# Taking the branch to a rarely used part behind the last scatter, with its flag copied there by GpSimd

## The chip, the cores and the metric

The kernel runs on one core of one Trainium2 chip. The metric is the device time of one execution in microseconds, taken as the median of several runs. The core has five engines that run their own instruction streams and wait for each other by semaphores: TensorE (PE; its weight loads are shown as PEld), VectorE (DVE), ScalarE (ACT), GpSimd (POOL) and SyncE (SP). A name with a q, such as POOLq, is that engine's sequencer: the part that takes instructions in order, waits for semaphores, loads registers, branches, and hands the rest to the engine.

## The reference, cut to what matters

A causal convolution of seven taps runs over 8 sequences of 2880 tokens with 192 features, with weights from a softmax for each of 8 heads. Its 23040 result rows go through a mixture of experts: each token picks one of 4 groups and one of the group's 4 experts by the largest logit, and is put through that expert alone.

```python
for k in range(K):                       # K = 7 taps, w = softmax(weight) per head
    out[b, s] += w[h, k] * x_pad[b, s + k]
g_idx = argmax(x @ w_group); e_idx = argmax(xg @ w_expert[g])
h  = maximum(xg[mask_e] @ w1[g, e], 0.0) # 192 -> 1024
ye = h @ w2[g, e]                        # 1024 -> 192
out[tok_idx] = combined[:, None] * ye    # weight of group times weight of expert
```

## The kernel before, in words

The first stage goes over the tokens in 18 units of 4 to 12 blocks of 120 tokens. For each unit TensorE does the convolution with a banded matrix and the router's logits; VectorE picks the expert, counts each token's place in its expert's list and builds the list; GpSimd writes the list to a table in DRAM with an indirect DMA (`idtab`), and ScalarE's queue writes the convolved rows (`xcd`).

The second stage works in slots of 256 tokens of one expert. For each slot GpSimd gathers the rows by an indirect DMA (`gather`, line 653), TensorE turns them (`turn`), multiplies by the first matrix (`hidden`, line 684) and the second (`back`, lines 702 and 706); the operands are split into a high and a low part, which is work for ScalarE and VectorE (lines 618 to 634, 689 and 690; line 627 is on GpSimd in the tail). `finish` (lines 753 to 757) scales the result: ScalarE writes one part of `ys`, VectorE adds the other, and GpSimd scatters each half of a slot (128 rows) to the output by an indirect DMA. The list of slots, `plan`, has three portions of fixed slots and a tail of 18 entries (9 of 256 and 9 of 128 tokens) that a table, computed on the chip in `table`, fills with what is left over. 187 scatters run in all: 160 for the portions, 27 for the tail (`idpt`).

Should the tail's 18 entries not be enough, or a list overflow, a flag (`flagi`, written by VectorE in line 878) is set, and a part at the program's end does the rest. That part is under `tc.If`: two loops whose code for all engines stands behind the branch. With this data the flag is 0, and the branch skips it. Every engine has the branch in its own stream, and so loads the flag into a register by itself (a TENSOR_LOAD), compares and branches. On the other side of the branch, each engine raises its semaphores to the values that the skipped part would have left; on GpSimd that includes one instruction for the semaphores of its DMAs, INC_SWDGE_SEM. The program ends with a DRAIN on each engine and a barrier (line 1233).

The order within an engine's stream is made by a scheduler, save where the code pins it (`tc.keep_in_program_order`). In the code, the flag is loaded six plan entries before the end (line 1106), ahead of the loop's last entries; the streams that the scheduler makes have the load and the branch near the end of each engine's work, and GpSimd's last scatter stands behind the branch.

Of the kernel before, what the change touches and what calls it, by code (L numbers as in the profile page):

```python
# [13 lines left out]
I32 = mybir.dt.int32  # L14
# [18 lines left out]
OOB_WHY = "the table's entries are clamped by construction"  # L33
# [3 lines left out]
def conv_moe_kernel(  # L37
# [10 lines left out]
    nc = tc.nc  # L48
# [106 lines left out]
    const = ctx.enter_context(tc.tile_pool(name="const", bufs=1))  # L155
# [90 lines left out]
    def clear_table():  # L246
# [12 lines left out]
        out=tri, in_=ones, pattern=[[1, P]], compare_op=ALU.is_gt, fill=0.0, base=0, channel_multiplier=-1,  # L259
# [12 lines left out]
    for nb in sorted({n for _, n in units}):  # L272
# [35 lines left out]
        out=sel, in_=ident.rearrange("p (e l) -> p e l", e=E), axis=AX.X, op=ALU.add)  # L308
    nc.gpsimd.iota(io[:, 0:1], pattern=[[0, 1]], base=0, channel_multiplier=1)
    nc.vector.tensor_scalar(  # L310
        out=io[:, 1:2], in0=io[:, 0:1], scalar1=LE - 1, scalar2=None, op0=ALU.bitwise_and)
# [6 lines left out]
    for g in range(NSK):  # L318
        nc.sync.dma_start(
            out=skew[0:R, g * HG:(g + 1) * HG],  # L320
            in_=bass.AP(wvd.tensor, wvd.offset + VL - KS - (BT - 1) + g * HG * VL, [[1, R], [VL, HG], [1, VW]]),
# [13 lines left out]
    for h in range(H):  # L335
        nc.scalar.activation(
            out=band[0:R, h], in_=skew[0:R, h, BT - 1::-1], func=AF.Exp, bias=wm[0:R, h:h + 1],
# [338 lines left out]
    def hidden(W, X, f2, hook=lambda: None):  # L676
        xa, xb = X
        ah, al, bh, bl = (W[n] for n in ("ah", "al", "bh", "bl"))
        hp = ph.tile([P, 2, SLOT], F32, name="ph")
        for j in range(2):  # L680
            fs = slice((2 * f2 + j) * P, (2 * f2 + j + 1) * P)
            ops = ((ah, xa[:, 0]), (al, xa[:, 0]), (ah, xa[:, 1]), (bh, xb), (bl, xb))
            for i, (wgt, xx) in enumerate(ops):
                nc.tensor.matmul(out=hp[:, j], lhsT=wgt[:, fs], rhs=xx, start=i == 0, stop=i == len(ops) - 1)  # L684
            if j == 0:
                hook()
        hh = ff.tile([P, 2, SLOT], F32R, name="hh", bufs=HB)
        hl = ff.tile([P, 2, SLOT], F32R, name="hl", bufs=HB)
        nc.scalar.activation(out=hh, in_=hp, func=AF.Relu)  # L689
        nc.vector.scalar_tensor_tensor(  # L690
            out=hl, in0=hp, scalar=0.0, in1=hh.bitcast(F32), op0=ALU.max, op1=ALU.subtract,
        )
        return hh, hl
# [84 lines left out]
    flagi = const.tile([P, 2], I32, name="flagi")  # L778
# [166 lines left out]
    def advance(rate):  # L945
        credit[0] += rate
        while credit[0] >= 1.0:
            credit[0] -= 1.0
            step()

    tab = [None]
    nrare = [None]
# [55 lines left out]
    plan = [(pi, e, s) for pi, (_, spe) in enumerate(portions) for e in range(E) for s in range(spe)]  # L1008
# [9 lines left out]
    def tiles(i):  # L1018

        return 1 if plan[i][0] == "tail" and plan[i][1] >= NBIG else 2  # L1020
# [74 lines left out]
    def later(lag, f):  # L1095

        pend.append((tick + lag, f))
        pend.sort(key=lambda a: a[0])
# [3 lines left out]
            pend.pop(0)[1]()  # L1102

    for i, (pi, e, s) in enumerate(plan):
        if i == len(plan) - 6:
            nrare[0] = nc.values_load(
                flagi[0:1, 1:2], min_val=0, max_val=1, skip_runtime_bounds_check_because=OOB_WHY)
        W, ids = opened[i]
        n = tiles(i)
        oo = [po.tile([P, 512], F32, name="po") for _ in range(n)]  # L1110
        steps = NF // 2 if n == 2 else 2
        for f2 in range(steps):
            last = f2 == steps - 1
            if n == 2:
                HH = hidden(W, turned[i], f2, lambda: advance(rate[0]))
                advance(rate[0])

                def fold(W=W, oo=oo, HH=HH, f2=f2, ids=ids, xs=gathered[i], last=last):
                    back(W, oo, HH, f2, lambda: advance(rate[0]))
                    if last:  # L1120
                        finish(oo, ids, xs)

                later(LAG - last, fold)
            else:
                hr = hidden_small(W, turned[i], f2)

                def fold(W=W, oo=oo, hr=hr, f2=f2, ids=ids, xs=gathered[i], last=last):
                    HH = turn_small(hr)

                    def fold2():  # L1130
                        back_small(W, oo, HH, f2)
                        if last:
                            finish(oo, ids, xs)

                    later(LAG_S, fold2)

                later(0.5, fold)
            if f2 == 0:
                open_slot(i + 2)
            for q in range(f2, NF // 2, steps):  # L1140
                k = (q + 2) % 4
                if q < 2:
                    split_one(W, k)
                elif i + 1 < len(plan):
                    split_one(opened[i + 1][0], k)
            if i + 1 < len(plan):
                if f2 == n - 1:
                    turned[i + 1] = turn(gathered[i + 1], tiles(i + 1))
            drain(tick)
            tick += 1  # L1150
# [2 lines left out]
        drain(tick)  # L1153


    with tc.If(nrare[0] != 0):
        nover = nc.values_load(
            flagi[0:1, 0:1], min_val=0, max_val=1, skip_runtime_bounds_check_because=OOB_WHY)
        with tc.For_i(0, nover, 1):
            for u in range(NU):  # L1160
                c0, nb = units[u]
                ee = rt.tile([P, UB, E], F32, name="dd")[0:BT, 0:nb]
                gi = rt.tile([P, 2, UB], I32, name="posi", bufs=1)[0:BT, :, 0:nb]
                gb = rt.tile([P, 2, UB], F32, name="posb")[0:BT, :, 0:nb]
                gr = rt.tile([P, UB], F32, name="posr", bufs=1)[0:BT, 0:nb]
                idw = rt.tile([P, LH], I32, name="lsi")[0:BT, 0:nb]
                pn = posn[0:BT, c0:c0 + nb]
                va = vals[0:BT, 0:nb]
                nc.vector.tensor_copy(out=gi[:, 1], in_=pn)
                nc.vector.tensor_scalar(  # L1170
                    out=gi[:, 0], in0=gi[:, 1], scalar1=VS.bit_length() - 1, scalar2=None, op0=ALU.logical_shift_right)
                nc.vector.tensor_scalar(out=gi[:, 1], in0=gi[:, 1], scalar1=VS - 1, scalar2=None, op0=ALU.bitwise_and)
                nc.vector.tensor_copy(out=gb, in_=gi)
                nc.vector.tensor_scalar(out=gb[:, 0], in0=gb[:, 0], scalar1=float(VS), scalar2=-1.0, op0=ALU.mult, op1=ALU.add)
                nc.vector.tensor_tensor(
                    out=ee, in0=eoff[0:BT].unsqueeze(1).broadcast_to([BT, nb, E]),
                    in1=gb[:, 0].unsqueeze(2).broadcast_to([BT, nb, E]), op=ALU.is_equal,
                )
                nc.vector.tensor_tensor(
                    out=ee, in0=ee, in1=ends[0:BT, u].unsqueeze(1).broadcast_to([BT, nb, E]), op=ALU.mult)  # L1180
                nc.vector.tensor_reduce(out=gr, in_=ee, axis=AX.X, op=ALU.add)
                nc.vector.tensor_tensor(out=gr, in0=gr, in1=gb[:, 1], op=ALU.add)
                nc.vector.tensor_copy(out=gi[:, 0], in_=gr)
                nc.vector.tensor_scalar(out=idw, in0=va, scalar1=float(c0 * BT - 1), scalar2=None, op0=ALU.add)
                for k in range(nb):
                    nc.gpsimd.indirect_dma_start(
                        out=idtab[:, :], out_offset=bass.IndirectOffsetOnAxis(ap=gi[:, 0, k:k + 1].bitcast(U32), axis=0),
                        in_=idw[:, k:k + 1], in_offset=None,
                    )
            for _ in table(ebase, 0, 0):  # L1190
                pass
        nend[0] = nc.values_load(
            tab[0][0:1, 0, 3:4], min_val=NTAIL, max_val=NTAB, skip_runtime_bounds_check_because=OOB_WHY,
        )
        with tc.For_i(NTAIL, nend[0], 1) as i:
            r1, r2, row = tail_regs(lambda c: tab[0][0:1, bass.ds(i, 1), c:c + 1], 3)
            W = weights(r1, r2)
            ids = ff.tile([P, 2, 1], I32, name="idt", bufs=1)
            tail_ids(row, ids)
            while W["todo"]:  # L1200
                split_one(W)
            xs = gather(ids, N)
            X = turn(xs)
            oo = [po.tile([P, 512], F32, name="po") for _ in range(2)]
            HHs = []
            for f2 in range(NF // 2):
                HHs.append(hidden(W, X, f2))
                if f2:
                    back(W, oo, HHs[f2 - 1], f2 - 1)
            back(W, oo, HHs[-1], NF // 2 - 1)  # L1210
            finish(oo, ids, xs)
# [25 lines left out]
```

## Time and profile before

| what | value |
|---|---|
| median of 3 runs | 1174.79 us (1172.58 to 1176.51) |
| the profiled execution's own time | 1170.84 us |
| its span, first to last instruction | 1169.0 us |
| mean granted TensorE clock | 0.977 |
| TensorE busy | 1111.7 us (95%) |
| VectorE, ScalarE, GpSimd busy | 69%, 59%, 43% |
| last stretch without any matmul | 1155 to 1169 us |

Engine times in the profile do not count what the sequencers do: register loads, branches, semaphore steps and drains. Those are listed only in the view of a source line, each as queue, operation, count, duration in ns (least, median, greatest), and the first and last start in us. The end of this kernel has to be read from there, since the busy engines are done by then. Spans on GpSimd are rough.

### The profile page before, as it was taken

To read this page: it belongs to the slowest core of one execution; us is meant where nothing else is said; L and a number is where in the kernel's file an instruction comes from. 1 tells how busy PE (TensorE), PEld (TensorE's weight loads), DVE (VectorE), ACT (ScalarE), POOL (GpSimd) and SP (SyncE) were. 2 spreads that over 40 slices of the span, in tenths; PEclk is the share of its full clock that TensorE was granted. 3 is DMA by queue.
4 is the path that set the end of the run, shared out by engine and by line. 5 is a ranking of instruction groups with operands and counts; after the bars stand their busy time and mean duration, and the time that the engine had idled before them with its cause. 6 is when DMAs were issued, how large, how long until landed. Compare 5 with 4: busy or idle time off the path is not lost.

```text
span 1169.0 us, 23803 instructions
## 1 busy us (share of the span) xinstructions
PE 1111.7 (95%) x8468; PEld 1079.3 (92%) x8468; DVE 804.5 (69%) x1668; ACT 690.1 (59%) x1374; POOL 498.2 (43%) x443
## 2 busy tenths in 40 slices
PE   5887999999999999999999999999999999999994
PEld 4766999998999999999999999999999999998984
DVE  4756788887877676666678565656565656688772
ACT  5544677657655555656554555555555656677772
POOL 2103234434434343434344444444444445578771
PEclk8879999999999999999999999999999999999997
DMA  8766699989775654546354574545454545599960
GB/s 228 217 182 178 173 213 230 226 203 268 217 194 143 165 156 118 143 116 170 95 162 95 155 203 128 142 128 141 130 141 128 140 118 167 146 243 266 248 160 19
DMA packets 167212, 195.63 MB, mean 167 GB/s; under 512 B 22500, under 2 KB 144333, under 8 KB 167086
## 3 DMA queue, kind: packets, MB, share of 16 engines
q1 hardware_dynamic: 125006, 140.41, 44.6%
q0 software_dynamic: 18752, 35.85, 10.5%
q10 hardware_dynamic: 23328, 17.80, 6.2%
q8 instruction: 67, 1.10, 0.4%
q14 instruction: 59, 0.48, 0.1%
HBM read 158.79 MB, written 36.58 MB: 167 GB/s over the span
## 4 chain that ended last, share of the span: by engine, by line
PE 79%; DVE 5%; DMA 4%; issue 3%; ACT 3%; another core or an unknown queue 0%; POOL 0%; POOLq 0%; ACTq 0%; DVEq 0%; SPq 0%
PE ph L684 33%; PE po L702 21%; PE po L706 10%; PE pm L409 3%; DMA xg<-xcd,idpt 3%; PE pm L451 2%; PE pm L666 2%; PE pm L667 2%; PE pm L428 1%; PE ph L719 1%; PE pm L448 1%; DVE hl L690 1%; DVE ohl L549 1%; DMA idtab<-lsi,rowi 1%; ACT cw L633 1%
## 5 line engine op out<-in xcount | busy, mean ns | idle before, releaser
L702 PE MATMUL po<-cw,hh 128*128 128x384 f32 x1424 | 443.4, 369 | 5.9 <-DVE ys L754 5.9
L684 PE MATMUL ph<-xa,ah 128*128 128x256 f32 x1424 | 390.2, 296 | 1.9 <-DVE xa L669 1.5
L757 POOL DMA_INDIRECT out<-ys,idp x160 | 167.8, 1049 | 447.4 <-DVE ys L754 348.8
L706 PE MATMUL po<-cw,hl 128*128 128x192 f32 x1424 | 357.3, 251 | 0.0
L690 DVE SCALAR_TENSOR_TENSOR hl<-ph,hh 128x512 fp32r<-128x512 f32 x356 | 241.2, 686 | 163.5 <-ACT hh L689 149.3
L689 ACT ACTIVATE hh<-ph 128x512 fp32r<-128x512 f32 x356 | 210.8, 594 | 205.8 <-PE ph L684 170.2
L702 PEld LDWEIGHTS po<-cw,hh 128*128 128x128 f32 x1424 | 268.6, 189 | 9.7 <-DVE ys L754 7.6
L684 PEld LDWEIGHTS ph<-xa,ah 128*128 128x128 f32 x1424 | 271.0, 190 | 5.0 <-DVE xa L669 1.6
L706 PEld LDWEIGHTS po<-cw,hl 128*128 128x128 f32 x1424 | 272.6, 191 | 1.5
L653 POOL DMA_INDIRECT xg<-xcd,idp x160 | 190.0, 1187 | 62.0 <-issue 29.6
L684 PE MATMUL ph<-xb,bh 128*128 128x256 f32 x712 | 201.9, 284 | 0.3 <-DVE xb L673 0.3
L684 PE MATMUL ph<-xb,bl 128*128 128x256 f32 x712 | 201.8, 283 | 0.0
L684 PE MATMUL ph<-xa,al 128*128 128x256 f32 x712 | 201.3, 283 | 0.0
L684 PEld LDWEIGHTS ph<-xa,al 128*128 128x128 f32 x712 | 136.5, 192 | 2.1
L684 PEld LDWEIGHTS ph<-xb,bl 128*128 128x128 f32 x712 | 136.7, 192 | 0.0
L684 PEld LDWEIGHTS ph<-xb,bh 128*128 128x128 f32 x712 | 136.2, 191 | 0.4 <-DVE xb L673 0.4
L634 DVE TENSOR_TENSOR cw<-rawc,cw 128x768 fp32r<-128x768 f32 x114 | 105.3, 953 | 18.3 <-ACT cw L633 13.7
L619 DVE TENSOR_TENSOR al<-raw,ah 128x1024 fp32r<-128x1024 f32 x57 | 70.5, 1238 | 38.8 <-ACT ah L618 21.6
L754 DVE SCALAR_TENSOR_TENSOR ys<-po,xg,ys 128x192 f32<-128x192 f32 x187 | 76.2, 416 | 23.2 <-ACT ys L753 18.1
L633 ACT ACTIVATE cw<-rawc 128x768 fp32r<-128x768 f32 x114 | 91.0, 837 | 1.8 <-DMA rawc<-in_moe_w 1.4
L672 ACT ACTIVATE xb<-pm 64x256 fp32r<-64x256 f32 x98 | 36.0, 367 | 93.4 <-DVE xa L669 86.2
L753 ACT ACTIVATE ys<-po,xg 128x192 f32<-128x192 f32 x187 | 75.8, 418 | 22.2 <-PE po L706 12.0
(216 smaller groups left out, 1561.0 us busy)
## 6 DMA issues: line engine op xcount, KB each, us to landing
rawc<-in_moe_w SPq DMA_DIRECT2D x114, 384.0 KB
raw<-in_moe_w SPq DMA_DIRECT2D x57, 512.0 KB
raw<-in_moe_w SPq DMA_DIRECT2D x114, 256.0 KB
xcd<-xc ACTq DMA_DIRECT2D x13, 1085.6 KB
xin<-in_x SPq DMA_DIRECT2D x7, 1134.0 KB
xc<-in_moe_w SPq DMA_DIRECT2D x18, 384.0 KB
xin<-in_x SPq DMA_DIRECT2D x6, 1039.5 KB
xin<-in_moe_w SPq DMA_DIRECT2D x9, 512.0 KB
```

The source lines that it names most:

```text
L619: eng.get(k, nc.vector).tensor_tensor(out=al, in0=ra, in1=ah.bitcast(F32), op=ALU.subtract)
L633: pin(PINW, nc.scalar.activation(out=cw[:, fs, 0, :], in_=rc[k - 2], func=AF.Copy))
L634: eng.get(k, nc.vector).tensor_tensor(out=cw[:, fs, 1, :], in0=rc[k - 2], in1=cw[:, fs, 0, :].bitcast(F32), op=ALU.subtract,)
L653: nc.gpsimd.indirect_dma_start(out=xs[:, t, :], out_offset=None, in_=xcd[0:known, :], in_offset=bass.IndirectOffsetOnAxis(ap=ids[:, t, 0:1 ...
L684: nc.tensor.matmul(out=hp[:, j], lhsT=wgt[:, fs], rhs=xx, start=i == 0, stop=i == len(ops) - 1)
L689: nc.scalar.activation(out=hh, in_=hp, func=AF.Relu)
L690: nc.vector.scalar_tensor_tensor(out=hl, in0=hp, scalar=0.0, in1=hh.bitcast(F32), op0=ALU.max, op1=ALU.subtract,)
L702: nc.tensor.matmul(out=oo[t][:, 0:2 * D], lhsT=hh[:, j, ts], rhs=cw[:, f].rearrange("p a d -> p (a d)"), start=f == 0, stop=False,)
L706: nc.tensor.matmul(out=oo[t][:, 0:D], lhsT=hl[:, j, ts], rhs=cw[:, f, 0, :], start=False, stop=f == NF - 1,)
L753: nc.scalar.activation(out=ys[:, t, :], in_=oo[t][:, D:2 * D], func=AF.Copy, scale=g)
L754: nc.vector.scalar_tensor_tensor(out=ys[:, t, :], in0=oo[t][:, 0:D], scalar=g, in1=ys[:, t, :], op0=ALU.mult, op1=ALU.add,)
L757: nc.gpsimd.indirect_dma_start(out=outviews[nscat[0] % len(outviews)], out_offset=bass.IndirectOffsetOnAxis(ap=ids[:, t, 0:1].bitcast(U32) ...
```

## The change

Two lines go and three come. The flag is no longer loaded six entries before the end. Behind the loop, GpSimd copies the first row of `flagi` (two numbers) into a tile of its own, `flagl`; the copy is pinned in program order, which on GpSimd puts it behind the loop's last scatter. All five engines then load the flag from `flagl`, so each load needs the copy's semaphore. The branch, the part behind it and the end of the program are as they were.

```diff
     for i, (pi, e, s) in enumerate(plan):
-        if i == len(plan) - 6:
-            nrare[0] = nc.values_load(
-                flagi[0:1, 1:2], min_val=0, max_val=1, skip_runtime_bounds_check_because=OOB_WHY)
         W, ids = opened[i]
...
+    flagl = const.tile([1, 2], I32, name="flagl")
+    tc.keep_in_program_order(nc.gpsimd.tensor_copy(out=flagl, in_=flagi[0:1]))
+    nrare[0] = nc.values_load(flagl[0:1, 1:2], min_val=0, max_val=1, skip_runtime_bounds_check_because=OOB_WHY)
     with tc.If(nrare[0] != 0):
```

GpSimd's stream around the branch, as a difference (`-` before, `+` now). `bl` is a low part of the tail's weights, `out<-ys,idpt` a scatter of the tail, line 1157 the first instruction of the rarely used part:

```order
 L627 TENSOR_TENSOR bl<-xin,bh 128x1024
 L627 TENSOR_TENSOR bl<-raw,bh 128x1024
-L757 DMA out<-ys,idpt 23040x192 x5
-L1106 TENSOR_LOAD flagi
+L757 DMA out<-ys,idpt 23040x192 x6
+L1154 COPY flagl<-flagi 1x2
+L1155 TENSOR_LOAD flagl
 L1156 COMPARE_AND_BRANCH
 L1157 TENSOR_LOAD flagi
```

All six last scatters now stand ahead of the branch, with the copy and the load between. The other piece of GpSimd's stream is its end, on the branch's other side (the first row is INC_SWDGE_SEM):

```order
 L1156 ISA
 L1156 UNCONDITIONAL_BRANCH
-L757 DMA out<-ys,idpt 23040x192
-L1233 UNCONDITIONAL_BRANCH
 L1233 ISA
```

The sixth scatter stood here, and is gone from here. On VectorE the load and the branch stay behind the last `ys`, and the load reads the other tile:

```order
 L731 TENSOR_TENSOR hl<-pm,hh 128x512
 L754 SCALAR_TENSOR_TENSOR ys<-po,xg_202,ys 128x192
-L1106 TENSOR_LOAD flagi
+L1155 TENSOR_LOAD flagl
 L1156 COMPARE_AND_BRANCH
 L1157 TENSOR_LOAD flagi
```

Nothing of VectorE's work is moved there; the other engines' streams differ in the same way. Apart from this, one small instruction moves in the whole program: near the tail's table, VectorE's cast of line 874 goes ahead of an operation of line 690 and one of line 669.

## The prediction

> **What bounds the kernel now.** I read the page first: TensorE is busy almost everywhere, so the middle of the kernel is its matmuls, and this change touches none of them. What matters is what stands behind the last matmul. The view that sums busy time by stretch shows it.
>
> ```profile
> PE 1111.7 (95%) x8468; PEld 1079.3 (92%) x8468; DVE 804.5 (69%) x1668; ACT 690.1 (59%) x1374; POOL 498.2 (43%) x443
> ...
> 1146.00:1155.00 9.00, 7.94 (x53) 7.31 (x52) 2.64 (x5) 3.54 (x7) 1.94 (x2) 1.00 0.06 19
> 1155.00:1169.00 14.00, 0.00 (x0) 0.00 (x0) 0.00 (x0) 0.00 (x0) 0.97 (x1) 0.55 0.02 6
> ```
>
> In the last 14.0 us no matmul, vector or activation instruction runs; only one GpSimd instruction does, 0.97 us long. The timeline says which (start, length, engine, line), with the last matmuls and two of the VectorE results that the scatters write out:
>
> ```profile
> 1150.93 0.42 DVE L754 SCALAR_TENSOR_TENSOR ys<-po,xg,ys 128x192 f32<-128x192 f32 x1 [0.79 <-ACT ys L753]
> 1151.62 0.97 POOL L757 DMA_INDIRECT out<-ys,idpt  x1 [7.95 <-DVE ys L754]
> 1152.90 0.97 POOL L757 DMA_INDIRECT out<-ys,idpt  x1 [0.30 <-DVE hl L731]
> 1153.36 0.58 PE L745 MATMUL po<-cw,hl 128*128 128x192 f32 x4
> 1154.43 0.42 DVE L754 SCALAR_TENSOR_TENSOR ys<-po,xg,ys 128x192 f32<-128x192 f32 x1 [1.56 <-ACT ys L753]
> 1160.24 0.97 POOL L757 DMA_INDIRECT out<-ys,idpt  x1 [6.37 <-DMA out<-ys,idpt]
> ```
>
> The last ys is complete at 1154.85, and its scatter starts 5.39 us later. For what lies between, the views of the flag's tile, of line 1106 (its load), 1156 (branch and its untaken side) and 1233 (end of the program) list the sequencers' instructions: queue, operation, count, ns min/median/max, first and last start.
>
> ```profile
> L878 DVE CAST flagi<-flags x1: 161/161/161, 626.5 to 626.5; 128x2 int32<-128x2 f32 x1
> L1106 SPq TENSOR_LOAD <-flagi x1: 276/276/276, 1126.6 to 1126.6; - x1
> L1106 POOLq TENSOR_LOAD <-flagi x1: 505/505/505, 1152.0 to 1152.0; - x1
> L1106 DVEq TENSOR_LOAD <-flagi x1: 547/547/547, 1154.4 to 1154.4; - x1
> ...
> L1156 POOLq EVENT_SEMAPHORE  x6: 17/30/43, 1155.3 to 1157.4; - x6
> L1156 ACTq EVENT_SEMAPHORE  x2: 17/17/17, 1155.0 to 1155.1; - x2
> L1156 DVEq EVENT_SEMAPHORE  x2: 21/21/21, 1158.4 to 1158.5; - x2
> L1156 POOLq COMPARE_BRANCH  x1: 53/53/53, 1152.6 to 1152.6; - x1
> L1156 ACTq COMPARE_BRANCH  x1: 45/45/45, 1154.5 to 1154.5; - x1
> L1156 DVEq COMPARE_BRANCH  x1: 72/72/72, 1155.1 to 1155.1; - x1
> L1156 POOLq INC_SWDGE_SEM  x1: 1855/1855/1855, 1157.5 to 1157.5; - x1
> ...
> L1233 POOLq EVENT_SEMAPHORE  x4: 17/17/17, 1168.2 to 1168.9; - x4
> L1233 POOLq DRAIN  x3: 46/109/8133, 1160.0 to 1168.7; - x3
> L1233 SPq DRAIN  x3: 7/7/13, 1163.1 to 1168.4; - x3
> ```
>
> GpSimd's tail reads: flag load 1152.0, branch 1152.6, first instruction on the branch's other side only at 1155.3 (2.6 us after the branch ended), six semaphore steps to 1157.5, INC_SWDGE_SEM to 1159.3, then the last scatter, which stands behind the branch in GpSimd's program, and a DRAIN of 8.133 us from 1160.0 to 1168.1. From there to the end of the span it is 0.9 us. So the end is set by GpSimd's sequencer, and more than half of its 14 us is one DRAIN.
>
> **What the DRAIN waits for** decides the case. SyncE passed all its own end waits, the last scatter's landing among them, by 1163.1, so the scatter's data were down 5.0 us before GpSimd's DRAIN ended. Nor are the GpSimd cores busy after a scatter: a tensor operation starts 0.02 us behind an indirect DMA (1128.24 + 1.46 = 1129.70).
>
> ```profile
> L757 POOL DMA_INDIRECT out<-ys,idp x160 | 167.8, 1049 | 447.4 <-DVE ys L754 348.8
> L653 POOL DMA_INDIRECT xg<-xcd,idp x160 | 190.0, 1187 | 62.0 <-issue 29.6
> ...
> 1128.24 1.46 POOL L653 DMA_INDIRECT xg<-xcd,idpt  x1 [0.30 <-issue]
> 1129.72 2.40 POOL L627 TENSOR_TENSOR bl<-xin,bh 128x1024 fp32r<-128x1024 f32 x1
> ...
> L1225 POOLq INC_SWDGE_SEM  x1: 27/27/27, 0.2 to 0.2; - x1
> L1225 POOLq DRAIN  x1: 184/184/184, 0.4 to 0.4; - x1
> L1225 POOL MEMSET const-uint8-127<- x1: 115/115/115, 0.4 to 0.4; 128x1 uint8 x1
> ```
>
> The same two instructions at the start of the program, before any DMA of GpSimd's, take 27 and 184 ns, against 1,855 and 8,133 at the end. Both have grown with something that the kernel left behind, and hundreds of GpSimd's DMAs lie between (the two groups of 160 alone). My reading is that the long DRAIN works through the record of all of them and does not care when the last was issued. This is inferred, not shown.
>
> **The change, part by part.** *Removed*: the last scatter no longer waits behind branch, semaphores and INC_SWDGE_SEM. It starts 0.27 us after its ys, as the scatter at 1151.62 did (1150.93 + 0.42 = 1151.35): 1155.1, issued by 1156.1, that is 5.1 us earlier than the 1161.2 of before. It stays one DMA, past no other transfer.
>
> *Added*: one GpSimd copy of 1x2. The nearest rows are these; I take 0.2 us, the iota's 0.13 would do too.
>
> ```profile
> L347 POOL COPY wrb<-wr 64x20 f32<-64x20 f32 x1 | 0.2, 190 | 0.0
> L309 POOL IOTA lts<- 128x1 int32 x1 | 0.1, 133 | 3.8 <-DVE vals L293 3.8
> ```
>
> *Moved*: the flag load on all five queues. Before, each loaded a flag that stood ready from about 626.7 us on, so SyncE branched at 1127 and GpSimd at 1152.6, while the last 1.3 us of matmuls (to 1153.94) still ran. Now every load waits for the copy. Behind it on TensorE, ScalarE, VectorE and SyncE stands only the branch, semaphore steps and the closing barrier, no work, so their delay costs nothing unless it outlasts GpSimd's. VectorE, which took longest from branch to other side (1155.1 to 1158.4, 3.2 us), would be there by 1160.4 and needs 0.3 us more.
>
> *GpSimd's new chain*, from 1154.85: 0.27 to the scatter, 0.97 to issue it (1156.1); copy 0.2 (1156.3); 0.1 for the semaphore, an estimate; load 0.505 and 0.1 to the branch with its 0.053 (1157.0); 2.6 to the other side (1159.6); six semaphore steps at 0.1 apiece, the spacing of VectorE's two (1160.2). The old 2.2 us there held a wait, as I read it for a scatter in flight: the one of 1152.90 was down by 1157.4 at the latest, 4.5 us after its start. The new last scatter, started at 1155.1, would by the same 4.5 us be down at 1159.6, hidden behind copy, load and branch; without that cover it would cost those 4.5 us less the 1.0 of its issue, 3.5. Then INC_SWDGE_SEM 1.855 (1162.1), the DRAIN D, and 0.9: the end is 1163.0 + D.
>
> The 2.6 us behind the branch could be a one-time mishap, since ScalarE needed only 0.4 (1154.5 to 1155.0); with 0.4 the end would come 2.2 us sooner. I keep 2.6, because GpSimd and VectorE both show it. The Trainium skill, "Runtime: NRT & Kernel Launch", section "Instruction fetch mechanics", says that a taken branch to a target outside the two pages held must first fetch it by DMA. By that rule the stall recurs wherever the branch is put, which speaks against the change: placed before the last scatter it was partly under matmuls, behind it it is bare; the sum by the rule is the one with 2.6, without it 2.2 us less.
>
> *D*: the upper end is the row as it stands, 8.1, if the DRAIN works from its start. The lower end is 5.0, the part that lies behind the last moment at which the scatter can still have been in flight. I take 6.9, from the end of the scatter's issue (1161.2) to 1168.1: the DRAIN at the start of the program also ended just behind the memset ahead of it (0.4 + 0.115 against 0.4 + 0.184), so it first lets the engine finish. The end is 1163.0 + 6.9 = 1169.9, against 1169.0: **0.9 us later**. With D = 8.1 it is +2.1, with 5.0 it is -1.0. So the scatter is through 5.1 us sooner, and nothing comes of it, because the DRAIN now has INC_SWDGE_SEM in front of it, which is through at 1162.1, where before it had the scatter, through at 1161.2.
>
> *A side effect*: on VectorE one cast of the tail's table (line 874, 128x4) moves ahead of two split operations of line 690 and 669 near 628 us.
>
> ```profile
> L874 DVE CAST tb_ei<-tb_e x1: 159/159/159, 629.0 to 629.0; 128x4 int32<-128x4 f32 x1
> ```
>
> At worst TensorE waits 0.16 us once. I count it as nothing, as it stands among idle time of VectorE (69% busy).
>
> **The rivals.** (1) *The DRAIN belongs to the last scatter.* If it ends a fixed 6.9 us after the last scatter's issue, it now ends at 1156.1 + 6.9 = 1163.0, behind INC_SWDGE_SEM (1162.1), and the span at 1163.9: 5.1 us faster, 1169.7 by the median. For it: in the run of before the two stand side by side. Against it: the landing by 1163.1 and the free cores. With the 184 ns of the first DRAIN the end would be 1163.2, 5.8 faster, 1169.0. The Trainium skill, "VectorE: DVE Perf Modes", section "The DRAIN you can't avoid", calls the boilerplate DRAIN a constant of about 12 ns on all engines; by that rule the end would be 1163.0, 6.0 faster. The row of 8,133 ns disagrees with it.
>
> (2) *The two fetches queue up.* VectorE and GpSimd now branch at the same moment instead of 2.5 us apart. If both targets come through one path in turn, GpSimd's 2.6 us stand behind VectorE's 3.2, and with D = 8.1 the end is 1163.0 + 3.2 + 8.1 = 1174.3: 5.3 us slower, 1180.1. It decides from about 1.4 us of queueing on with D = 8.1 (2.1 + 1.4 = 3.5). For it: SyncE's and GpSimd's branches were spread by 28 us and never met. Against: ScalarE's target was there in 0.4 us while GpSimd's was still out, until 1155.3.
>
> (3) *The change does nothing at the end* because another engine's tail takes over. SyncE's end waits need INC_SWDGE_SEM's semaphores, 1162.1, and then some 0.7 us; that stays under any D over 1. I give it no chance of its own.
>
> **How the numbers follow.** The profiled execution took 1170.84 us (span 1169.0 and 1.84 around it); it lies 3.95 us below the median of the three runs (1174.79) and 1.7 below the lowest. I carry the difference over: 1174.79 + 0.9 = 1175.7, and the profiled execution 1171.7. The forecast, with D from 5.0 to 8.1, has a chance of 0.71 and a range of its own of 1173.5 to 1178 (its ends -1.0 and +2.1, and 0.5 to 1 us for medians of runs that themselves spread from 1172.58 to 1176.51). Rival (1) has 0.19, rival (2) 0.10. The range over all is 1169 to 1180: it takes in rival (1) and all but the end of (2). About 0.3% (3.5 us) is what a measurement of this kernel can tell from no change; by it the chances are those of the cases: faster 0.19, within 0.71, slower 0.10.
>
> **What would show it.** In the profile of the changed kernel the last scatter should start near 1155.1 on a span like this one, 0.3 us behind the last ys; the copy right behind it; GpSimd's branch at about 1157.0 and its first step on the other side 2.6 us later; INC_SWDGE_SEM again near 1.9 us. The DRAIN is the test: if it still takes 5 to 8 us although the scatter landed before it began, the reading holds; if it is under 2 us, rival (1) is right and the kernel is faster. A gap behind GpSimd's branch of over 4 us would be rival (2). If GpSimd reaches its untaken side in 0.4 us, the forecast is 2.2 us too high.

## The result, and the profile after

The changed kernel takes 1179.26 us (median of 15 runs, 1172.86 to 1187.15) against 1173.41 us for the kernel before (15 runs, 1169.95 to 1177.75): the ratio is 1.0053, with a 95% interval from 1.0032 to 1.0074. It is slower by about 0.5%, which is more than the 0.3% that a measurement can tell from no change. The profiled execution took 1179.22 us, with a span of 1177.5.

The same two stretches of the view by stretch, cut at the last `ys` as in the prediction (busy time of PE, PEld, DVE, ACT, POOL, then clock, DMA share, GB/s):

```profile
1152.40:1161.40 9.00, 7.94 (x54) 7.31 (x52) 2.64 (x5) 3.54 (x7) 1.94 (x2) 1.00 0.05 16
1161.40:1177.50 16.10, 0.00 (x0) 0.00 (x0) 0.00 (x0) 0.00 (x0) 1.14 (x2) 0.58 0.02 7
```

The last stretch with work on TensorE is what it was. The stretch without any has grown from 14.0 to 16.1 us, with two GpSimd instructions in it instead of one. The timeline shows which (start, length, engine, line), behind the last `ys`:

```profile
1160.84 0.42 DVE L754 SCALAR_TENSOR_TENSOR ys<-po,xg,ys 128x192 f32<-128x192 f32 x1 [1.57 <-ACT ys L753]
1161.53 0.97 POOL L757 DMA_INDIRECT out<-ys,idpt  x1 [1.27 <-DVE ys L754]
1162.49 0.17 POOL L1154 COPY flagl<-flagi 1x2 int32<-1x2 int32 x1
```

The scatter follows its `ys` by 0.27 us, where it was 5.39 before. The views of lines 1155 (load), 1156 (branch) and 1233 (end) show what takes its place (queue, operation, count, ns least/median/most, first and last start):

```profile
L1155 POOLq TENSOR_LOAD <-flagl x1: 697/697/697, 1162.7 to 1162.7; - x1
L1155 DVEq TENSOR_LOAD <-flagl x1: 679/679/679, 1162.7 to 1162.7; - x1
...
L1156 POOLq EVENT_SEMAPHORE  x6: 17/30/43, 1167.3 to 1167.7; - x6
L1156 DVEq EVENT_SEMAPHORE  x2: 21/21/21, 1167.3 to 1167.4; - x2
...
L1156 DVEq COMPARE_BRANCH  x1: 72/72/72, 1163.5 to 1163.5; - x1
L1156 POOLq COMPARE_BRANCH  x1: 53/53/53, 1163.5 to 1163.5; - x1
...
L1156 POOLq INC_SWDGE_SEM  x1: 1875/1875/1875, 1167.8 to 1167.8; - x1
...
L1233 POOLq DRAIN  x3: 46/103/6930, 1169.7 to 1177.2; - x3
```

All five engines load at 1162.7 and branch between 1163.0 and 1163.5. GpSimd and VectorE are both 3.7 to 3.8 us on the way to the other side, and then come GpSimd's INC_SWDGE_SEM (1.875) and a DRAIN of 6.930 us. From the end of the last `ys` (1161.26) to the end of the span this **tail** is 16.2 us, against 14.15 before: +2.1 us. That is a third of the 5.85 us between the medians. The rest lies earlier. The flag's cast, which stands at the end of the first stage, already starts 8.2 us later in this execution than in that of before (626.5):

```profile
L878 DVE CAST flagi<-flags x1: 162/162/162, 634.7 to 634.7; 128x2 int32<-128x2 f32 x1
```

### The profile page after: what moved, and what is told of

It reads as the page before. It is cut to its first block, busy times and chain, and to the rows that moved or that the text cites. A ratio compares the mean times of both kernels' runs of the same rounds, so it can differ in the third digit from the quotient of the medians.

```text
span 1177.5 us, 23804 instructions
## 1 busy us (share of the span) xinstructions
PE 1114.5 (95%) x8468; PEld 1081.6 (92%) x8468; DVE 804.8 (68%) x1668; ACT 689.9 (59%) x1374; POOL 498.9 (42%) x444
## 4 chain that ended last, share of the span: by engine, by line
PE 72%; DVE 7%; issue 4%; DMA 4%; ACT 4%; SPq 0%; POOL 0%; another core or an unknown queue 0%; ACTq 0%; DVEq 0%; POOLq 0%
PE ph L684 31%; PE po L702 20%; PE po L706 9%; PE pm L409 3%; PE pm L451 2%; DMA xg<-xcd,idpt 2%; DVE hl L690 2%; PE pm L667 1%; PE pm L666 1%; DMA idtab<-lsi,rowi 1%; PE pm L428 1%; DVE cw L634 1%; PE pm L448 1%; PE ph L719 1%; DVE ohl L549 1%
## 5 line engine op out<-in xcount | busy, mean ns | idle before, releaser
L757 POOL DMA_INDIRECT out<-ys,idp x160 | 170.3, 1064 | 448.5 <-DVE ys L754 340.0
```

Source lines behind the costliest of these rows:

```text
L757: nc.gpsimd.indirect_dma_start(out=outviews[nscat[0] % len(outviews)], out_offset=bass.IndirectOffsetOnAxis(ap=ids[:, t, 0:1].bitcast(U32) ...
```

## The experiments

The kernels ran in three groups on three chips; each is compared with runs of the kernel before on the same chip. "Tail" is always the time from the end of the last `ys` to the end of the span in the profiled execution.

**What else the change moves.** The prediction considered the order of the instructions only. The addresses of the tiles in the on-chip memory moved too; a pool is the stretch of it from which a group of tiles is allocated. The new tile `flagl` holds 8 bytes on one partition, takes 32 bytes in the pool of constants, and pushes all that stands behind it by 32. The pools' first addresses in the two programs, in bytes of a partition, with the remainder to 64:

```
pool (what stands in it)              before          after
pa   (list, tables)                   36160  (0)      36192 (32)
pa2  (xin input, xc convolved rows)   52736  (0)      52768 (32)
rt   (the router's small tiles)      108224  (0)     108256 (32)
wraw (weights as loaded)             119968 (32)     120000  (0)
wsp  (weights split)                 141472 (32)     141504  (0)
ff   (activations, ys)               198816 (32)     198848  (0)
```

Four kernels take tail and shift apart; a fifth takes the wait for the copy out.

*same_layout*: the change, with the flag copied into a tile that is no longer needed, so that no tile moves.

```diff
-    flagl = const.tile([1, 2], I32, name="flagl")
+    flagl = prioi[0:1, 0:2]
```

> The change as it is, but the copied flag lies in an old tile (prioi, done with since the program's start) and no new tile is made, so every tile stands at its address of before. Theory A (the change costs 2.1 us behind the last ys, 14.1 us before and 16.2 now, and the other 3.8 us of the 5.9 us between the medians come from the new tile, which moves most tiles by 32 bytes): ratio to before 1.0018, and 16.2 us from the last ys to the end. Theory B (the late branch or the pinned copy itself slows the work ahead): ratio 1.005 as measured for the change. Theory C (the 3.8 us are chance between builds): anything from 1.000 to 1.005 with no link to the addresses.

Measured: 1169.41 us against 1164.87, 1.0040 [1.0017, 1.0063]; tail 16.3, with 3.81 us behind GpSimd's branch and the DRAIN again 6.930. The tail is the changed kernel's, so it doesn't depend on the addresses. The ratio lies between what the two theories gave and decides nothing by itself.

*shift_only*: the branch as before, and the new tile there, written only in the part that is skipped.

```diff
+    flagl = const.tile([1, 2], I32, name="flagl")
     with tc.If(nrare[0] != 0):
+        nc.gpsimd.tensor_copy(out=flagl, in_=flagi[0:1])
```

> The kernel before with its early branch; the new tile is made all the same, and written only in the rarely used part, which does not run. Tiles stand at the addresses that they have with the change. Theory A: ratio 1.0032 (3.8 us), with 14.1 us behind the last ys, as before. Theory B: ratio 1.000. Theory C: no telling.

Measured: 1172.05 against 1164.87, 1.0073 [1.0045, 1.0100], with a tail of 14.2 as before. So 32 bytes that nothing uses make the kernel slower, by more than either theory had. Up to the branch every engine has the same instructions in the same order as before, and only addresses differ; so it is in aligned and front_shift below. Both kernels were then measured side by side on another chip, with one that shifts only the second stage's tiles.

*after_again* is the changed kernel as it is, *shift_again* is shift_only once more.

> The changed kernel as it is, on the chip on which the next kernels run, so that all of them have one measure. If the change's cost is its longer tail (+2.1 us) and the 32-byte shift of the tiles (+3 to +8 us), the ratio is 1.004 to 1.009, and the tail behind the last ys is again 16.2 us. If the first measured 1.0053 belonged to that chip, it comes out within 1.002.

> Only the 32-byte shift of the tiles, with the branch where it was before. If tail and shift add up, it lies about 2 us (0.0018) under the changed kernel on this chip, with a tail of 14.2 us. If the shift has no cost of its own, the ratio is 1.000, and the first measured 1.0073 was chance.

Measured on that chip, with before at 1165.15: the change 1174.01, 1.0067 [1.0044, 1.0089], tail 16.6; the shift alone 1169.23, 1.0035 [1.0015, 1.0056], tail 13.8. Within these intervals they add up as expected: the shift is 4.1 us, and the change lies another 0.0032 (3.7 us) above it, against 2.8 us between the two tails.

*aligned*: before, with a filler of 32 bytes behind the first stage's pools, so that `pa`, `pa2` and `rt` stay at multiples of 64 and `wraw`, `wsp` and `ff` come to them.

```diff
     with tc.If(nrare[0] != 0):
+        fil = rt.tile([P, 2], I32, name="fil", bufs=1)
+        nc.gpsimd.tensor_copy(out=fil[0:1], in_=flagi[0:1])
```

> Before, with a tile of 32 bytes added behind the first stage's pools (written only in the untaken part): the first stage's tiles stay at multiples of 64 bytes, and the second stage's (weights, split weights, activations) move from 32 behind such a multiple to one. It tells which half of the shift costs. Theory A, the first stage's tiles cost it, where the gap between the two profiles opens: this is not slower than before, 0.998 to 1.001. Theory B, the second stage's tiles cost it: slower by the same 1.004 to 1.007 as with the whole shift. Tail 14.2 us by both.

Measured: 1162.65 against 1165.15, 0.9983 [0.9965, 1.0001]. The second stage's tiles don't cost it; whether their new place gains a little, the interval leaves open.

*front_shift*: both fillers, so that `wraw`, `wsp` and `ff` are at 32 as before and only the first stage's pools have a new remainder.

```diff
+    flagl = const.tile([1, 2], I32, name="flagl")
     with tc.If(nrare[0] != 0):
+        fil = rt.tile([P, 2], I32, name="fil", bufs=1)
+        nc.gpsimd.tensor_copy(out=fil[0:1], in_=flagi[0:1])
+        nc.gpsimd.tensor_copy(out=flagl, in_=flagi[0:1])
```

> Before, with two tiles of 32 bytes (written only in the untaken part), so that the first stage's tiles stand 32 bytes behind a multiple of 64 as in the changed kernel, and the second stage's at 32 as before. Theory A, the first stage's tiles cost it: slower by 1.0035 to 1.007, as with the whole shift, and the rows of 768 bytes on ScalarE's and SyncE's queues take 46 to 48 ns in the first 60 us instead of 43 to 44. Theory B, only both halves together cost it: within 0.998 to 1.002. Tail 14.2 us by both.

Measured: 1172.14 against 1163.68, 1.0074 [1.0049, 1.0099], tail 13.8. With this the shift is placed: it is the first stage's pools, by 0.35 to 0.74% in three measurements, 4 to 8.5 us. The profile says when it is lost. The flag's cast ends the first stage's work; its row in aligned, and then in front_shift:

```profile
L878 DVE CAST flagi<-flags x1: 162/162/162, 625.8 to 625.8; 128x2 int32<-128x2 f32 x1
```

```profile
L878 DVE CAST flagi<-flags x1: 162/162/162, 629.8 to 629.8; 128x2 int32<-128x2 f32 x1
```

Over the profiled executions the cast starts at 622.3 to 626.5 us where the first stage's pools are at multiples of 64, and at 626.1 to 634.7 where they are 32 behind, so that the two groups touch (few_scatters, described below, moves less and is left out: 616.2). A mark halfway through the first stage parts them, the 25th of the 35 operations of line 549, which build the list. Its row in aligned, and then in front_shift:

```profile
295.63 0.95 DVE L549 TENSOR_TENSOR ohl<-iop,posb 120x768 f16<-120x768 f32 x1
```

```profile
302.60 0.95 DVE L549 TENSOR_TENSOR ohl<-iop,posb 120x768 f16<-120x768 f32 x1
```

It starts at 295.0 to 296.5 us in the six executions at multiples of 64 and at 297.4 to 304.0 in the seven that are 32 behind, no_rare and after_mid_drain among them (one execution of each run). From there to the cast it is 327 to 331 us in both groups, and from the cast to the last `ys` 525 to 528. So the loss falls into the first 300 us, where the DMA share is 0.82 to 0.86 in before, the change, aligned and front_shift, against 0.53 to 0.54 in the next 300. Nothing is added or made good later.

*Why* these 32 bytes cost time is not settled. It isn't the engines' own work: the convolution's matmuls (line 409) and the longest VectorE operation of the list (line 549) take as long in the changed kernel as before. Nor is it the granted clock, which is 0.93 to 0.95 up to 300 us in the one group and 0.93 to 0.94 in the other. The rows of before, then of the change:

```profile
L549 DVE TENSOR_TENSOR ohl<-iop,posb x35: 418/951/961, 32.0 to 614.7; 120x768 f16<-120x768 f32 x30, 120x256 f16<-120x256 f32 x4, 120x512 f16<-120x512 f32 x1
...
L409 PE MATMUL pm<-xin,band x198: 324/406/836, 9.2 to 551.5; 126*120 126x288 f32 x168, 126*120 126x192 f32 x24, 126*120 126x96 f32 x6
```

```profile
L549 DVE TENSOR_TENSOR ohl<-iop,posb x35: 416/951/965, 33.3 to 622.8; 120x768 f16<-120x768 f32 x30, 120x256 f16<-120x256 f32 x4, 120x512 f16<-120x512 f32 x1
...
L409 PE MATMUL pm<-xin,band x198: 324/406/835, 9.1 to 559.5; 126*120 126x288 f32 x168, 126*120 126x192 f32 x24, 126*120 126x96 f32 x6
```

Something points at the transfers. In the first 60 us SyncE's queue (q1) moves the same 11,694 packets in every kernel, the input rows and the first weights, and the view of the DMA queues in that window gives the share of the 16 engines' time that they took. Before, the change, and front_shift:

```profile
q1 hardware_dynamic: 11694, 11.29, 68.1%
```

```profile
q1 hardware_dynamic: 11694, 11.29, 74.7%
```

```profile
q1 hardware_dynamic: 11694, 11.29, 77.2%
```

The seven executions with the first stage's pools at multiples of 64 have 66.5 to 71.2%, the seven others 72.0 to 77.2%. The rows of 768 bytes on this queue took 42.8 to 45.5 ns on average in the one group and 46.2 to 50.5 in the other (43.3 before, 50.5 in front_shift, where 46 to 48 was expected). On ScalarE's queue, of which the same was expected, the rows did not get longer (49.8 ns in front_shift, 51.9 before). At a DMA share of 0.83 (before) to 0.87 (front_shift) in that window, longer packets can delay the work. But the two groups lie close together, longer packets can also be the mark of a busier queue, and this goes along with the loss without being shown to cause it. The input tile `xin` starts at a multiple of 256 bytes before, and 32 behind one in the changed kernel, and its rows are 768 bytes, three times 256. The Trainium skill, "DMA: Bandwidth & Descriptors", section "How a descriptor splits into AXI transactions", says that a descriptor is split into pieces of 256 bytes, and that the first piece of one which does not start at a multiple of 256 starts at the multiple below, with bytes that are not used; the section states this of reads, and `xin` is written. No run here tells a start off 256 from a start off 64, nor `xin` from its neighbours: a shift by 64 bytes was not tried.

**What the tail is made of.** *scatter_first*: the last scatter ahead of the branch, as in the change, but with no copy: only GpSimd's load of the flag is queued behind the scatter, the other engines load `flagi` whenever they come to it.

```diff
-            nc.gpsimd.indirect_dma_start(
+            lastsc[0] = nc.gpsimd.indirect_dma_start(
...
+    with tc.issue_after(lastsc[0].ins):
+        nrare[0] = nc.values_load(flagi[0:1, 1:2], min_val=0, max_val=1, skip_runtime_bounds_check_because=OOB_WHY)
```

> The last scatter ahead of the branch without the copy: GpSimd's load of the flag is queued behind the last scatter, all engines load flagi, addresses as before. Theory A: from the last ys on 0.2 us to GpSimd's load, 0.7 for it, 0.1, 3.7 to the other side (fetched together with VectorE's), 0.5, 1.9, 6.9, 0.9: 14.9 us against 14.1, that is 0.8 us later than before (ratio 1.0007) and 1.3 us sooner than with the copy. If GpSimd's scatter alone set the end (rival 1 of the prediction): 5.1 us sooner, ratio 0.9957.

Measured: 1165.14 against 1164.87, 1.0008 [0.9989, 1.0027], tail 13.8 (expected 14.9). GpSimd's sequencer loads the flag while the engine still issues the scatter, so the branch is at 0.61 us behind the last `ys`; in the change, with the copy between, it is at 2.2. The other side is reached 2.9 us after the branch. The views of line 1155, of the branch and of the program's end:

```profile
L1155 POOLq TENSOR_LOAD <-flagi x1: 502/502/502, 1149.6 to 1149.6; - x1
...
L1156 POOLq EVENT_SEMAPHORE  x6: 17/30/43, 1153.1 to 1153.6; - x6
...
L1156 DVEq EVENT_SEMAPHORE  x2: 21/21/21, 1153.1 to 1153.2; - x2
...
L1156 DVEq COMPARE_BRANCH  x1: 72/72/72, 1149.8 to 1149.8; - x1
L1156 POOLq COMPARE_BRANCH  x1: 53/53/53, 1150.2 to 1150.2; - x1
...
L1233 POOLq DRAIN  x3: 46/103/6930, 1155.6 to 1163.1; - x3
```

The load takes 502 ns and not 697: in this kernel the five loads don't come at once. The way behind the branch is shorter too. With VectorE and GpSimd branching within 0.03 us of each other, and all five engines within 0.5 (the change, after_again, same_layout, after_mid_drain), GpSimd needs 3.7 to 4.1 us and VectorE 3.8 to 4.2. With VectorE 0.4 us ahead (scatter_first, best) they need 2.7 to 2.9 and 3.1 to 3.3, and with VectorE some 2.5 us behind (before and all kernels with its branch) 2.5 to 2.7 and 3.0 to 3.3. In scatter_first and best the two ways still overlap for the whole of GpSimd's, and that makes GpSimd's at most 0.4 us longer and VectorE's no longer. So the meeting of these two alone does not make the 1.1 us; which of the five engines' branches does is not separated.

**What the DRAIN works on.** *mid_drain*: before, and one more DRAIN of GpSimd's, pinned behind the 184th of the 187 scatters.

```diff
             nscat[0] += 1
+            if nscat[0] == 184:
+                tc.keep_in_program_order(nc.gpsimd.drain())
```

> The kernel before, with one more DRAIN on GpSimd behind its 184th of 187 scatters, where it then idles for 8 us. If the long DRAIN works through a record of all of GpSimd's DMAs since the start: the added DRAIN takes some 6.9 us and the waiting for its last scatter, the last DRAIN ends within 0.5 us of the last scatter's landing, INC_SWDGE_SEM falls from 1.86 to under 0.4 us, and the end comes 5.5 to 8 us sooner (ratio 0.993 to 0.995). If the DRAIN belongs to the last scatter or to the program's end: the last DRAIN still ends 6.9 us behind the scatter's issue, and the ratio is 1.000 or more.

Measured: 1159.42 against 1164.87, 0.9957 [0.9936, 0.9978] (expected 0.993 to 0.995): faster than before, and by the ratios than the change. The tail is 7.2 us. The added DRAIN (line 764), INC_SWDGE_SEM and the closing DRAIN:

```profile
L764 POOLq DRAIN  x1: 7908/7908/7908, 1136.0 to 1136.0; - x1
...
L1158 POOLq INC_SWDGE_SEM  x1: 240/240/240, 1150.7 to 1150.7; - x1
...
L1235 POOLq DRAIN  x3: 46/109/2617, 1151.6 to 1155.3; - x3
```

The long DRAIN now stands at 1136.0 to 1143.9, where GpSimd waits 7.95 us for the next `ys` anyway. The one at the end takes 2.6 us, and INC_SWDGE_SEM 0.24 instead of 1.86. The added DRAIN ends 6.7 us behind the issue of its scatter, nearly as long as the closing one of before. So the work is not tied to the program's end; it is done once, by the first DRAIN that comes.

*few_scatters*: the 160 scatters of the three portions are left out, and with them those rows of the output.

```diff
-            nc.gpsimd.indirect_dma_start(
+            if nscat[0] >= 160: nc.gpsimd.indirect_dma_start(
```

> Before, with the 160 scatters of the three portions left out (their rows of the output are not written; the tail's 27 are). It has 239 of some 399 GpSimd DMAs. If the closing DRAIN and INC_SWDGE_SEM work through the record of all of them, in proportion, the DRAIN's part behind the last scatter's issue is 6.93 x 239/399 = 4.2 us and INC_SWDGE_SEM 1.1 us. If the length depends on the kinds or queues in use and not on the count, they stay at 6.9 and 1.9.

Measured: INC_SWDGE_SEM 0.780 us, and a DRAIN that ends 2.53 us behind the last scatter's issue (1147.20), instead of 6.94 (expected in proportion: 1.1 and 4.2).

```profile
L1156 POOLq INC_SWDGE_SEM  x1: 780/780/780, 1144.6 to 1144.6; - x1
...
L1233 POOLq DRAIN  x3: 46/109/3727, 1146.0 to 1150.3; - x3
1146.23 0.97 POOL L757 DMA_INDIRECT out<-ys,idpt  x1 [4.93 <-DVEq L1156]
```

Both fall with the scatters left out, and by more than in proportion to all 399 DMAs: the 160 carry 4.4 us of the DRAIN, 27.5 ns apiece, and 1.08 us of INC_SWDGE_SEM, 7 ns apiece. Only scatters were left out; whether the gathers and the list's writes count too, and so how the rest of the time divides, these runs don't tell.

*no_rare*: the rarely used part and its branch are left out, and INC_SWDGE_SEM goes with them.

```diff
-    with tc.If(nrare[0] != 0):
-        nover = nc.values_load(
...
-            finish(oo, ids, xs)
```

> Before, without the rarely used part and its branch (with this data the part does nothing). If the long DRAIN comes from the record of GpSimd's DMAs, it stays at 6.9 us behind the last scatter's issue, and the tail is 0.3 + 1.0 + 6.9 + 0.9 = 9.1 us against 14.2. If it belongs to the branch and its semaphores, it falls under 3 us and the tail under 5. All its tiles stand 32 bytes behind a multiple of 64, so that its whole time is not compared.

Measured: a DRAIN that again ends 6.94 us behind the last scatter's issue (1158.14), and a tail of 9.0 (one run).

```profile
1157.17 0.97 POOL L757 DMA_INDIRECT out<-ys,idpt  x1 [1.27 <-DVE ys L754]
...
L1174 POOLq DRAIN  x3: 46/103/8138, 1156.9 to 1165.6; - x3
```

The length is the same without any branch. The branch costs the tail 5.2 us (14.15 - 9.0) for itself, its semaphores and INC_SWDGE_SEM.

*after_mid_drain*: the changed kernel with the added DRAIN.

```diff
             nscat[0] += 1
+            if nscat[0] == 184:
+                tc.keep_in_program_order(nc.gpsimd.drain())
```

> The changed kernel with a DRAIN behind the 184th scatter. If the length of the last DRAIN goes by the DMAs issued since the one before it, and not by where the branch stands, it takes 1.4 us and INC_SWDGE_SEM 0.24 here too, and the tail is 16.3 - 5.5 - 1.6 = 9.2 us; the branch behind the scatter then still costs 2.0 us against the 7.2 us of before with this DRAIN. If the branch's other side adds something of its own to the DRAIN, it stays above 3 us.

Measured: tail 8.5 (expected 9.2), with INC_SWDGE_SEM 0.260 and a last DRAIN of 0.294 (one run of 1161.92 us, beside a median of 1163.68 for before). The last DRAIN is shorter than the 1.4 us expected: in mid_drain it stood directly at the last scatter, here 5.7 us behind its issue. So it seems that about 1.4 us pass behind a scatter just issued before a DRAIN can end, and that they pass under the branch here. Against mid_drain's 7.2 the change's place for the branch still costs 1.4 us.

*best*: mid_drain, scatter_first and aligned together.

> Three things together: a DRAIN of GpSimd's behind the 184th scatter, the last scatter ahead of the branch with the flag loaded behind it (no copy), and a filler tile of 32 bytes that puts the second stage's tiles at multiples of 64 and leaves the first stage's where they are. The tail: branch 0.61 behind the last ys, 2.9 to the other side, 0.6 for the semaphore steps, INC_SWDGE_SEM 0.24, the last DRAIN 1.4 to 1.9 from there, 0.85 to the end, together 6.7 to 7.1 us against 14.2, so -7.3; with -2 for the alignment the ratio is 0.992, and 0.994 if the alignment gives nothing. If the DRAIN's cost only moves to where it now stands, 1.000.

Measured: 1157.15 us against 1163.68, 0.9941 [0.9912, 0.9970] (expected 0.992 to 0.994), tail 5.7 us (expected 6.7 to 7.1). The last DRAIN is again 0.294:

```profile
L1158 POOLq INC_SWDGE_SEM  x1: 260/260/260, 1153.4 to 1153.4; - x1
...
L1237 POOLq DRAIN  x3: 46/103/294, 1153.7 to 1155.0; - x3
```

It is faster than the kernel before and, by the ratios, than the changed one. That it also beats mid_drain (0.9957 on another chip) the intervals don't show; the tail is 1.4 us shorter.

## Why the prediction was right or wrong

**The forecast.** 1175.7 was 3.6 us below the median, and the forecast's own range of 1173.5 to 1178 did not hold it. The range over all, 1169 to 1180, did, and that was luck: its upper end was there for rival (2), and 3.8 of the 5.85 us lie outside the tail, where no case of the prediction had anything. The likeliest case, no change by 0.3%, didn't come. The change is slower, to which the prediction gave 0.10, and that through a rival with another mechanism.

**The tail, term by term**, from the end of the last `ys`, predicted and measured: scatter 0.27 and 0.27; its issue 0.97 and 0.97; copy 0.2 and 0.17; semaphore 0.1 and 0.03; load 0.505 and 0.70; to the branch and its own time 0.1 and 0.13; to the other side 2.6 and 3.73; six steps 0.6 and 0.54; INC_SWDGE_SEM 1.855 and 1.875; DRAIN 6.9 and 6.93; to the end 0.9 and 0.85. The sum was 15.0 and is 16.2, so +0.9 became +2.1. The mechanism of the tail was right, and **the mis-sized term is the 2.6 us to the other side**, which measured 3.73, with the load as a smaller one (+0.2).

**The DRAIN.** The reading held: "works through the record of all of them and does not care when the last was issued". In the changed kernel it starts 8.2 us after the last scatter did and takes 6.93 us; mid_drain shows that the record is worked off by an earlier DRAIN, few_scatters that the length goes with the scatters that were issued, no_rare that the branch plays no part. That it is a record is the reading's picture; the runs show the lengths and what they go with. "All of them" was too simple as to shares, as few_scatters shows. 6.9 from between 5.0 and 8.1 was the right choice. Rival (1), a DRAIN that belongs to the last scatter, is refuted by the same row. The rule of about 12 ns on all engines (the Trainium skill, "VectorE: DVE Perf Modes", section "The DRAIN you can't avoid", which states it for the boilerplate around a program) fits SyncE's DRAINs of 7 to 13 ns here and not GpSimd's, which is an instruction of this program.

**The fetch.** The stall recurs behind the branch, as the prediction took it, in every profiled run that has the branch: GpSimd and VectorE stall for 2.5 to 4.2 us, SyncE for 0.47, ScalarE for 0.43 and TensorE for 0.06 to 0.12. In the changed kernel the view of the DMA queues from 1163.5 to 1167.3 us shows five transfers of instructions (queue: packets, MB, share of the 16 engines), as many as engines that branch:

```profile
q14 instruction: 4, 0.03, 3.0%
q8 instruction: 1, 0.02, 1.6%
```

This agrees with the Trainium skill, "Runtime: NRT & Kernel Launch", section "Instruction fetch mechanics", by which a taken branch out of the pages held forces a fetch of its target by DMA.

Rival (2), the two fetches queueing up, had a longer way right, but by some 1.1 us and not by VectorE's whole 3.2. One path taken in turn is not what the runs show, since in scatter_first and best the two ways overlap almost without cost. What the 1.1 us are is open. They are a term of the tail and not a case of their own. (The 28 us that the prediction gives in favour of this rival lie between SyncE's branch and VectorE's; between SyncE's and GpSimd's it is 25.6.)

**What failed** is the sentence that "the middle of the kernel is its matmuls, and this change touches none of them", and with it the side effects, of which only the moved cast was counted. The change touched the address of every tile behind the constants, and the loss from it falls where the matmuls do not fill the time: before, TensorE is busy for 266.9 of the first 300 us and for 296.8 of the next 300. By the experiments the shift costs 4 to 8.5 us and the tail 2.1 to 2.8, together 6 to 11; the change measured 5.85 us by the medians in the result, just below that sum, and 7.8 by the ratio on the second chip, in its lower part. Of the 3.8 us of the result that don't lie in the tail, the shift is the cause that was tested; the cast's place wasn't tested by itself, but same_layout has it too and its cast of the flag came at 623.6.

**How it would show**: the scatter 0.3 us behind the last `ys`, the copy right behind it, and the DRAIN of 5 to 8 us came as written. The gap behind the branch stayed just under the 4 us that were set as the sign of rival (2) (3.73), and passed it once in a later run (4.1).

## What to carry to other kernels

A new tile, however small and however rarely used, moves every tile that is allocated behind it: compare the addresses along with the order of the instructions, and put a small tile where nothing stands behind it or reuse a dead one. On GpSimd a DRAIN takes longer the more scatters have been issued since the last one; where hundreds of its DMAs stand before the program's end, an earlier DRAIN in a gap in which GpSimd waits anyway takes most of that out of the tail (7 us of 1165 by the tail of mid_drain, 5 by its time). What stands behind the last matmul counts in full, so keep copies and loads that could be done earlier out of the chain behind the last scatter, and the engines' branches apart: where all five came at once, GpSimd's was 1.1 us longer.

## What the hardware showed that was not expected

- 32 bytes of shift of the first stage's tiles cost 0.35 to 0.74%, lost in the first 300 us, with the matmuls of line 409 and VectorE's operation of line 549 as long as before; what in it costs is open.
- GpSimd's closing DRAIN takes 6.94 us with 187 scatters and 2.53 with 27, both counted from the last scatter's issue; with three scatters since the DRAIN before, 1.42 directly behind a scatter and 0.294 a few us later. INC_SWDGE_SEM goes with it: 1.86, 0.78, and 0.24 to 0.26 us.
- Five engines that load the same flag at once need 0.28 (SyncE) to 0.70 us (GpSimd); GpSimd alone needs 0.50.
- Behind a branch to a skipped part's end GpSimd stalls for 2.5 to 2.9 us when VectorE branches 0.4 us or more away from it, and for 3.7 to 4.1 when all five engines branch within 0.5 us.
